# Attention followed by mixture of depths: own code for the last batch's MoE, and fewer, larger loads for the first two batches

## The chip, the cores and the metric

The kernel runs on one core of a Trainium2 chip. A core has TensorE (PE: matrix products and transposes into PSUM), VectorE (DVE), ScalarE (ACT), GpSimd (POOL, which here issues every DMA) and SyncE (SP, unused here). The engines run their own instruction queues in order and wait for each other by semaphores. The metric is the device time of one execution in microseconds (us); lower is better.

## The reference, cut to what matters

Eight batches, twelve heads, 448 tokens, 64 columns a head. The attention has no softmax: relu, then square. Its output, 768 wide, goes into a mixture-of-depths layer: the 128 tokens of each batch with the highest gate score get a two-layer network added, the others pass.

```python
scores = scale * np.matmul(q, k.transpose(0, 1, 3, 2))      # q, k, v: [8, 12, 448, 64]
attn = np.maximum(scores, 0.0) ** 2 / S
x = np.matmul(attn, v)                                       # then [8, 448, 768]
...
scores = np.einsum('bsd,d->bs', x, w_gate)
for b in range(B):
    top_idx = np.argpartition(-scores[b], capacity)[:capacity]      # capacity 128
    xe = x[b, top_idx]
    h = np.maximum(xe @ w1, 0.0)                                     # w1 [768, 1024]
    ye = h @ w2                                                      # w2 [1024, 768]
    g = 1.0 / (1.0 + np.exp(-scores[b, top_idx]))
    out[b, top_idx] = x[b, top_idx] + g[:, None] * ye
```

## The kernel before

**Attention.** The work goes by head pairs: 48 of them, t = 0 to 47, six to a batch (hp = 0 to 5). For a pair, `transposes(t)` turns q and k on TensorE into the PSUM tile `t_ps`, and VectorE copies them to `qkt`; `scores(t, c)` makes four chunks of scores in `s_ps`; `relu_square(t, c)` takes a chunk through ScalarE (`r_sb`) and VectorE (`a_sb`); `attend(t, c)` multiplies by v into `o_ps`, and ScalarE copies the result, transposed, into `xT_sb`. In the loop the transposes of the next pair and the attend of the last one stand between the scores of this one.

**Mixture of depths.** Batch b-1 is ranked during the six pairs of batch b, in twelve half steps placed by the table `RANK`, and batch b-2 goes through its network by the table `FFN`. The ranking: `gate` (scores of all tokens, in `sc_ps`, copied to `bc`), `columns` (the same as columns, and their split in three bf16 pieces in `tok`), four `x_chunk` (x transposed back into `x_sb`; after the last one a DMA writes the whole batch to `out`), four `rank_chunk` on VectorE, `one_hot` (`hot`), `select` (`sel_ps`, then `sel`, `idx` and `g` on VectorE) and two `gather` halves (`xe_ps`, copied by ScalarE to `xeT`). The network: `hidden` (`h_ps`, relu to `hT`) and `project` (`ye_ps`, scaled by the gate into `gye`); then a DMA on GpSimd adds the 128 rows of `gye` to `out` at the rows `idx`. After the last pair the same steps run for batches 6 and 7 with no attention beside them.

**PSUM.** Eight banks: `s_ps` has two tiles of two banks, `t_ps`, `o_ps`, `ma_ps` and `mb_ps` one bank each. All steps of the ranking use `ma_ps` one after the other (only the second gather half uses `mb_ps`), all of the network `mb_ps`.

**Order.** Within an engine the attention and the MoE steps stand in the order of the code (`manual_schedule`). The instructions ahead of the loop on VectorE that only prepare constants (`wg_rep`, the gate's weights spread out; `slot_row`; `tie`, the tie-breaker of the ranking; `tok`) are put into VectorE's queue by the framework, not by the code. GpSimd's queue holds every DMA in the order of the code; a DMA that it issues waits until the DMA eight places ahead of it has landed. `load(b + 2)` is issued at the first pair of batch b; the weights `w1_sb` and `w2_sb` are issued ahead of batch 2's loads.

**Loads.** q of some heads is one DMA; k and v are four DMAs each for any number of heads (even and odd heads, and the two halves of the tokens). The DMAs turn float32 into bf16.

Of the kernel before, what the change touches and what calls it, by code (L numbers as in the profile page):

```python
# [19 lines left out]
def kernel(  # L20
# [204 lines left out]
    def moe_rank(b):  # L225
        xTb = xT.pop(b)
# [80 lines left out]
    def moe_ffn(b, idx, g, xeT):  # L307
# [14 lines left out]
        def project(half, f0, f1):  # L322
            cols_d = slice(half * 384, half * 384 + 384)
            if f0 == 0:
                ps["y"] = mb_ps_pool.tile([CAP, 384], FP32, name="ye_ps", tag="m")
# [5 lines left out]
            if f1 == NF:  # L331
                nc.scalar.activation(out=gye[:, cols_d], in_=ps["y"], func=AF.Copy,  # L332
                                     scale=g[:, 0:1])
                if half == 1:
                    nc.gpsimd.indirect_dma_start(  # L335
                        out=out.rearrange("b s d -> (b s) d"),
                        out_offset=bass.IndirectOffsetOnAxis(ap=idx[:, :1], axis=0),
                        in_=gye, in_offset=None, element_offset=b * S * HD,
                        compute_op=ALU.add)

        return {"h": hidden, "y": project}


# [93 lines left out]
```

## Time and profile before

| | us |
|---|---|
| median of 3 runs (260.65 to 262.56) | 262.12 |
| the profiled execution's own time | 262.02 |
| its span, first to last instruction | 260.0 |
| so outside the span | 2.0 |
| TensorE busy, VectorE busy, ScalarE busy, GpSimd busy | 211.9, 180.8, 196.3, 93.4 |

The mean granted TensorE clock is 0.968 of full speed. Instants below are counted from the start of the span. Busy times overlap across engines, so they don't add up to the span; what a stage costs is read from what waits in it.

### The profile page before, as it was taken

The numbers are of one execution on the slowest core, as the hardware profiler recorded it, in microseconds if no ns is written. First come the engines' busy times: TensorE is split into PE (matmuls) and PEld (weight loads), VectorE is DVE, ScalarE is ACT, GpSimd is POOL, SyncE is SP. The second block draws the span as 40 slices with busy tenths as digits, with TensorE's granted clock in tenths as the row PEclk, the third lists the DMA queues.
The fourth block names the chain that finished last, engine by engine and source line by source line (L and its number), as shares of the span: only waits on it lengthen the run. The fifth ranks groups of instructions, "written<-read, shape, count | busy, mean of one in ns | idle before, by whom it ended". The sixth has DMA issues, their size and how long they took to land.

```text
span 260.0 us, 6204 instructions
## 1 busy us (share of the span) xinstructions
PE 211.9 (82%) x2496; PEld 128.0 (49%) x2496; DVE 180.8 (70%) x427; ACT 196.3 (76%) x306; POOL 93.4 (36%) x136
## 2 busy tenths in 40 slices
PE   1777795832989889998989898989899889988750
PEld 1343353411656445655565456546655556456630
DVE  4566879970478786889589958996798669847200
ACT  1667996950689989898989988898889889962320
POOL 8998998106473109200830074002000300020022
PEclk9988999995699999999999999999999999999997
DMA  3789999999999966995599549944102330153544
GB/s 41 90 84 110 160 159 149 211 204 193 196 227 279 191 222 80 189 117 212 70 185 128 210 62 173 151 159 87 32 3 115 105 58 0 63 159 55 212 61 61
DMA packets 41868, 34.20 MB, mean 132 GB/s; under 512 B 15089, under 2 KB 39153, under 8 KB 40945
## 3 DMA queue, kind: packets, MB, share of 16 engines
q0 software_dynamic: 41840, 33.83, 77.9%
q8 instruction: 19, 0.31, 0.5%
q14 instruction: 9, 0.07, 0.1%
HBM read 39.32 MB, written 14.16 MB: 206 GB/s over the span
## 4 chain that ended last, share of the span: by engine, by line
DVE 29%; PE 25%; DMA 14%; ACT 12%; POOL 12%; issue 5%; POOLq 1%; ACTq 0%
DVE a_sb L202 13%; ACT r_sb L201 11%; DMA k_sb<-in_k_dram 8%; DVE qkt L179 6%; PE xe_ps L297 5%; PE h_ps L316 4%; DMA q_sb<-in_q_dram 4%; DVE trash L273 4%; PE s_ps L189 4%; PE sc_ps L245 3%; DVE x_sb L268 3%; PE o_ps L213 3%; POOL k_sb L89 2%; DMA out_dram<-gye,idx 2%; POOL v_sb L92 2%
## 5 line engine op out<-in xcount | busy, mean ns | idle before, releaser
L201 ACT ACTIVATE r_sb<-s_ps 128x896 bf16<-128x896 f32 x192 | 147.5, 830 | 22.2 <-PE s_ps L193 13.7
L202 DVE TENSOR_TENSOR a_sb<-r_sb 128x896 bf16<-128x896 bf16 x192 | 104.3, 563 | 40.1 <-ACT r_sb L201 39.9
L189 PE MATMUL s_ps<-qkt 64*128 64x448 bf16 x288 | 47.0, 368 | 7.8 <-ACT r_sb L201 4.2
L213 PE MATMUL o_ps<-a_sb,v_sb 128*64 128x448 bf16 x384 | 49.8, 367 | 3.0 <-DVE a_sb L202 1.9
L179 DVE COPY qkt<-t_ps 128x960 bf16<-128x960 bf16 x48 | 31.3, 651 | 12.8 <-PE t_ps L174 12.6
L213 PEld LDWEIGHTS <-v_sb 128*64 128x64 bf16 x384 | 20.3, 110 | 29.9 <-issue 23.3
L270 POOL DMA_DIRECT2D out_dram<-x_sb x8 | 4.5, 561 | 78.9 <-DVE x_sb L268 78.4
L335 POOL DMA_INDIRECT out_dram<-gye,idx x8 | 13.4, 1674 | 43.5 <-ACT xeT L299 21.5
L219 ACT ACTIVATE xT_sb<-o_ps 128x448 bf16<-128x448 f32 x48 | 26.8, 559 | 2.3 <-PE o_ps L213 2.3
L316 PE MATMUL h_ps<-xeT,w_sb 128*128 128x128 bf16 x384 | 26.5, 219 | 1.3 <-ACT hT L320 0.7
L168 PE MATMUL t_ps<-ident,q_sb 112*64 112x112 bf16 x384 | 19.0, 221 | 10.2 <-DMA q_sb<-in_q_dram 10.2
L189 PEld LDWEIGHTS <-qkt 64*128 64x128 bf16 x288 | 11.4, 94 | 31.5 <-issue 18.0
L92 POOL DMA_DIRECT2D v_sb<-in_v_dram x24 | 18.5, 770 | 23.5 <-DMA q_sb<-in_q_dram 18.8
L168 PEld LDWEIGHTS <-q_sb 112*64 112x64 bf16 x384 | 16.9, 115 | 17.2 <-DMA q_sb<-in_q_dram 11.1
L329 PE MATMUL ye_ps<-w_sb,hT 128*128 128x384 bf16 x128 | 23.5, 327 | 2.1 <-ACT gye L332 1.1
L316 PEld LDWEIGHTS <-w_sb 128*128 128x128 bf16 x384 | 22.5, 98 | 5.1 <-issue 3.2
L174 PE MATMUL t_ps<-ident,k_sb 128*64 128x128 bf16 x384 | 21.4, 227 | 4.4 <-DMA k_sb<-in_k_dram 4.4
L89 POOL DMA_DIRECT2D v_sb<-in_v_dram x24 | 20.3, 845 | 12.6 <-issue 9.0
L273 DVE SCALAR_TENSOR_TENSOR trash<-bc,cols,tie 112x448 bf16<-112x448 f32 x32 | 21.7, 678 | 0.0
L265 PE MATMUL x_ps<-ident,xT_sb 128*112 128x128 bf16 x192 | 16.8, 224 | 5.6 <-DVE cols L256 5.5
L92 POOL DMA_DIRECT2D k_sb<-in_k_dram x24 | 20.0, 838 | 1.0 <-PE s_ps L193 0.6
L89 POOL DMA_DIRECT2D k_sb<-in_k_dram x24 | 20.1, 838 | 0.3 <-DMA v_sb<-in_v_dram 0.2
(54 smaller groups left out, 207.9 us busy)
## 6 DMA issues: line engine op xcount, KB each, us to landing
out_dram<-x_sb POOLq DMA_DIRECT2D x8, 1344.0 KB, 5.2
q_sb<-in_q_dram POOLq DMA_DIRECT2D x6, 672.0 KB, 9.5
w_sb<-in_moe_w_dram POOLq DMA_DIRECT2D x2, 1536.0 KB, 14.5
k_sb<-in_k_dram POOLq DMA_DIRECT2D x12, 192.0 KB, 10.5
v_sb<-in_v_dram POOLq DMA_DIRECT2D x12, 192.0 KB, 8.6
k_sb<-in_k_dram POOLq DMA_DIRECT2D x12, 144.0 KB, 10.3
v_sb<-in_v_dram POOLq DMA_DIRECT2D x12, 144.0 KB, 10.2
q_sb<-in_q_dram POOLq DMA_DIRECT2D x2, 336.0 KB, 4.9
```

Of the source, the lines that this page charges most:

```text
L89: nc.gpsimd.dma_start(out=t[0:64, hs, 0:lo, :], in_=src[b, hs, 0:64 * lo].rearrange("h (p c) d -> p h c d", c=lo))
L92: nc.gpsimd.dma_start(out=t[64:128, hs, 0:hi, :], in_=src[b, hs, 64 * lo:S].rearrange("h (p c) d -> p h c d", c=hi))
L168: nc.tensor.matmul(out=ps[64 * hh:64 * hh + 64, c * P:(c + 1) * P], lhsT=qs[:, h0 + hh, c, :], rhs=ident[:P, :P], is_transpose=True, start ...
L179: nc.vector.tensor_copy(out=sb, in_=ps)
L189: nc.tensor.matmul(out=ps[:, hh, :S], lhsT=sb[rows, S + c * 128:S + (c + 1) * 128], rhs=sb[rows, :S], start=True, stop=True)
L201: nc.scalar.activation(out=r[:, :n], in_=ps[:, :n, :S], func=AF.Relu)
L202: nc.vector.tensor_tensor(out=a[:, :n], in0=r[:, :n], in1=r[:, :n], op=ALU.mult)
L213: nc.tensor.matmul(out=o_ps[t][rows, :], lhsT=vs[:, 2 * hp + hh, c, :], rhs=a[:, hh if c < 3 else 0, :], start=(c == 0), stop=(c == 2), sk ...
L219: nc.scalar.activation(out=xT[b][:, hp, :], in_=o_ps.pop(t), func=AF.Copy, scale=o_scale)
L273: nc.vector.scalar_tensor_tensor(out=trash, in0=bc[:P, :], scalar=cols[:, c:c + 1], in1=tie[:, c, :], op0=ALU.subtract, op1=ALU.is_ge, acc ...
L316: nc.tensor.matmul(out=ps["h"][:, f % 4, :], lhsT=w1_sb[:, m, f * 128:(f + 1) * 128], rhs=xeT[:, m, :], start=(m == 0), stop=(m == NM - 1))
L329: nc.tensor.matmul(out=ps["y"], lhsT=hT[:, f, :], rhs=w2_sb[:, f, cols_d], start=(f == 0), stop=(f == NF - 1))
```

## The change

Three things. **The loads of the first two batches** are cut into fewer pieces: batch 0 in heads 0 to 1, 2 to 5 and 6 to 11 (before: 0 to 1, 2 to 3, 4 to 7, 8 to 11), batch 1 in one piece (before: two halves). **The last batch** leaves the tables: its gate, transposes, gather and network have functions of their own (`x_begin`, `x_end`, `gather_last`, `last`), which use the PSUM tiles that the attention has given up and mix batch 6's network with batch 7's ranking; the copies of x go to ScalarE as two of 1536 columns. **The gather halves** swap their banks for every batch: the first half now uses `mb_ps`, the second `ma_ps`, the bank that `select` has used just before. `pieces`, split off from `columns`, stands directly behind it in the loop.

```diff
-    load_q(0, 2, 4)
-    load_kv(k_sb, k, 0, 2, 4)
+    load_q(0, 2, 6)
+    load_kv(k_sb, k, 0, 2, 6)
     load_kv(v_sb, v, 0, 0, 2)
-    load_q(0, 4, 8)
-    load_kv(k_sb, k, 0, 4, 8)
-    load_kv(v_sb, v, 0, 2, 4)
-    load_kv(v_sb, v, 0, 4, 8)
-    load(0, 8, H)
+    load_kv(v_sb, v, 0, 2, 6)
+    load(0, 6, H)
     for i in range(1, NBUF):
         zero_halves(i)
-    load(1, 0, 6)
-
+    load(1, 0, H)
     wg_cols = const.tile([128, NM], BF16)
     nc.gpsimd.dma_start(out=wg_cols, in_=moe_w_gate.rearrange("(m p) -> p m", p=128))
-    load(1, 6, H)
...
         def gather(half):
-            xe = (ma_ps_pool, mb_ps_pool)[half].tile([128, 3, CAP], FP32, name="xe_ps", tag="m")
+            xe = (mb_ps_pool, ma_ps_pool)[half].tile([128, 3, CAP], FP32, name="xe_ps", tag="m")
...
+        def x_begin():
+            for i in range(2):
+                ps["x", i] = s_ps_pool.tile([P, 2, 1024], BF16, name="x_ps2", tag="s")
+                for u in range(2):
+                    for m in range(NM - 1):
+                        x_part(i, u, m)
+
+        def x_part(i, u, m):
+            c = 2 * i + u
+            nc.tensor.matmul(out=ps["x", i][:, u, m * 128:(m + 1) * 128],
+                             lhsT=xTb[:, m, c * P:(c + 1) * P], rhs=ident,
+                             is_transpose=True, start=(m == 0), stop=(m == NM - 1))
+
+        def x_end():
+            for i in range(2):
+                for u in range(2):
+                    x_part(i, u, NM - 1)
+                nc.scalar.copy(out=x_sb[:, 2 * i:2 * i + 2, :], in_=ps["x", i][:, :, :HD])
+            nc.gpsimd.dma_start(out=out[b].rearrange("(p c) d -> p c d", c=NC), in_=x_sb)
+
+        def gather_last():
+            for half, (pool, tag) in enumerate(((o_ps_pool, "o"), (t_ps_pool, "t"))):
...
+                (nc.scalar.copy if half == 0 else nc.vector.tensor_copy)(
+                    out=xeT[:, half * 3:half * 3 + 3, :], in_=xe)
...
+        def last():
+            nc.scalar.activation(out=g, in_=g, func=AF.Sigmoid)
+            for half in range(2):
+                h = s_ps_pool.tile([128, 4, CAP], FP32, name="h_ps2", tag="s")
+                for m0 in (0, 3):
+                    for ff in range(4):
+                        f = 4 * half + ff
+                        for m in range(m0, m0 + 3):
...
+                nc.scalar.activation(out=hT[:, f:f + 4, :], in_=h, func=AF.Relu)
+            y = [mb_ps_pool.tile([CAP, 384], FP32, name="y_ps2", tag="m"),
+                 t_ps_pool.tile([CAP, 384], FP32, name="y_ps3", tag="t")]
...
+            nc.scalar.activation(out=gye[:, :384], in_=y[0], func=AF.Copy, scale=g[:, 0:1])
+            nc.vector.tensor_scalar(out=gye[:, 384:], in0=y[1], scalar1=g[:, 0:1],
+                                    scalar2=None, op0=ALU.mult)
+            scatter()
...
+        last, prev = B - 1, B - 2
+        r, handed[last] = moe_rank(last)
+        f = moe_ffn(prev, *handed.pop(prev))
+        r["gate"](0, NM - 1)
+        r["x_begin"]()
         for c in (0, 1, 3, 2):
             attend(NT - 1, c)
-        for hs in range(12):
-            moe(B, hs)
-        ffn_steps[B - 1] = moe_ffn(B - 1, *handed.pop(B - 1))
-        for hs in range(12):
-            place(FFN, ffn_steps[B - 1], hs)
+        r["gate"](NM - 1, NM)
+        r["col"]()
+        for c in range(NC):
+            r["rank"](c)
+        r["hot"]()
+        r["x_end"]()
+        for i in range(8):
+            f["h"](i, *((mb_ps_pool, "m"), (t_ps_pool, "t"))[i // 4])
+        f["y"](0, 0, 8, mb_ps_pool)
+        r["pieces"]()
+        r["xe_last"]()
+        f["y"](1, 0, 8, ma_ps_pool)
+        r["sel"](o_ps_pool, "o")
+        moe_ffn(last, *handed.pop(last))["last"]()
```

GpSimd's queue at the second half of batch 1's loads, before (the sizes are partitions x heads x elements, `_97` to `_99` batch 1's tiles):

```order
L122 DMA wg_cols<-in_moe_w_gate_dram 128x6x1
L80 DMA q_sb_97<-in_q_dram 112x6x256
L89 DMA k_sb_98<-in_k_dram 64x3x256
L92 DMA k_sb_98<-in_k_dram 64x3x192
L89 DMA k_sb_98<-in_k_dram 64x3x192
L92 DMA k_sb_98<-in_k_dram 64x3x256
L89 DMA v_sb_99<-in_v_dram 64x3x256
L92 DMA v_sb_99<-in_v_dram 64x3x192
L89 DMA v_sb_99<-in_v_dram 64x3x192
L92 DMA v_sb_99<-in_v_dram 64x3x256
```

And the whole of batch 1's loads after:

```order
L80 DMA q_sb_97<-in_q_dram 112x12x256
L89 DMA k_sb_98<-in_k_dram 64x6x256
L92 DMA k_sb_98<-in_k_dram 64x6x192
L89 DMA k_sb_98<-in_k_dram 64x6x192
L92 DMA k_sb_98<-in_k_dram 64x6x256
L89 DMA v_sb_99<-in_v_dram 64x6x256
L92 DMA v_sb_99<-in_v_dram 64x6x192
L89 DMA v_sb_99<-in_v_dram 64x6x192
L92 DMA v_sb_99<-in_v_dram 64x6x256
L118 DMA wg_cols<-in_moe_w_gate_dram 128x6x1
```

The nine DMAs of a load now carry twelve heads, and `wg_cols` stands behind all of them, no longer between two halves. Ahead of `w1_sb` there are 37 DMAs in place of 55.

VectorE's queue around the first pair of batch 1, before (a line with x2 is two instructions; `qkt` marks a pair):

```order
L202 TENSOR_TENSOR a_sb<-r_sb 128x896 [waits Activation_49]
L128 COPY wg_rep<-wg_cols 128x768 [waits DMASW5_49]
L202 TENSOR_TENSOR a_sb<-r_sb 128x896 [waits Activation_49] x2
L179 COPY qkt<-t_ps 128x960 [waits PE_49]
L202 TENSOR_TENSOR a_sb<-r_sb 128x448 [waits Activation_49]
L202 TENSOR_TENSOR a_sb<-r_sb 128x896 [waits Activation_49] x2
L136 CAST slot_row<-slot_i 112x128 [waits Pool_49]
L202 TENSOR_TENSOR a_sb<-r_sb 128x896 [waits Activation_49]
L179 COPY qkt<-t_ps 128x960 [waits PE_49]
L256 COPY cols<-col_ps 112x4 [waits PE_49]
L142 TENSOR_SCALAR tie<-tie_i 112x1792 [waits Pool_49]
L152 CAST tok_193<-tok_i 112x4x2 [waits Pool_49]
```

And after, at the same pairs:

```order
L174 COPY qkt<-t_ps 128x960 [waits PE_49]
L197 TENSOR_TENSOR a_sb<-r_sb 128x448 [waits Activation_49]
L131 CAST slot_row<-slot_i 112x128 [waits Pool_49]
L197 TENSOR_TENSOR a_sb<-r_sb 128x896 [waits Activation_49]
L137 TENSOR_SCALAR tie<-tie_i 112x1792 [waits Pool_49]
L123 COPY wg_rep<-wg_cols 128x768 [waits DMASW4_49]
L147 CAST tok_175<-tok_i 112x4x2 [waits Pool_49]
L147 CAST tok_177<-tok_i 112x4x2
L197 TENSOR_TENSOR a_sb<-r_sb 128x896 [waits Activation_49] x2
L174 COPY qkt<-t_ps 128x960 [waits PE_49]
L251 COPY cols<-col_ps 112x4 [waits PE_49]
```

`wg_rep` and `tie` moved: `wg_rep` now comes one pair later, behind the last product of pair 6 and behind `tie`, which before stood two lines behind the copy of `qkt` of pair 8. The gate's first matmul, which on TensorE stands ahead of the scores of pair 7 in both kernels, reads `wg_rep`.

TensorE's queue at batch 6's gather, before (numbers tell the tiles apart):

```order
L189 MATMUL s_ps_4083<-qkt_4008 128x448 [waits Activation_49]
L189 LDWEIGHTS qkt_4008
L189 MATMUL s_ps_4083<-qkt_4008 128x448
L297 LDWEIGHTS x_sb_3686
L297 MATMUL xe_ps_4090<-hot_3692,x_sb_3686 128x128 [waits DVE_49]
```

And after, where the second gather half begins:

```order
L294 MATMUL xe_ps_4072<-hot_3674,x_sb_3668 128x128
L294 LDWEIGHTS x_sb_3668
L294 MATMUL xe_ps_4072<-hot_3674,x_sb_3668 128x128
L294 LDWEIGHTS x_sb_3668
L294 MATMUL xe_ps_4086<-hot_3674,x_sb_3668 128x128 [waits DVE_49]
```

The wait for VectorE's copy of `sel_ps` has moved from the first of the 24 gather matmuls to the thirteenth.

## Rows read from the trace of the kernel before

**Rows 1.** Windows view: busy time of each engine (xcount), clock, DMA share, GB/s.

```profile
3.00:18.00 15.00, 9.82 (x78) 4.45 (x80) 7.49 (x18) 7.51 (x11) 15.00 (x28) 1.00 0.79 87
18.00:39.00 21.00, 17.75 (x190) 8.98 (x187) 15.85 (x30) 19.22 (x30) 19.61 (x32) 0.92 1.20 137
...
42.00:49.00 7.00, 5.32 (x66) 2.94 (x65) 6.96 (x18) 4.57 (x8) 2.75 (x5) 1.00 1.12 209
...
59.00:64.40 5.40, 0.87 (x9) 0.50 (x9) 0.00 (x0) 0.00 (x0) 3.38 (x5) 0.50 1.50 193
```

**Rows 2.** Chain that ended last, 0 to 66 us: start, us, what.

```profile
7.48 0.52 POOL v_sb L89
...
38.29 0.80 POOL w_sb L155
...
42.12 0.66 POOL k_sb L92
...
43.38 20.93 DMA k_sb<-in_k_dram
```

**Rows 3.** Timeline at batch 2's first pair: start, us, engine, line, [idle before].

```profile
60.96 0.59 PE L168 MATMUL t_ps<-ident,q_sb 112*64 112x112 bf16 x8 [5.64 <-DMA q_sb<-in_q_dram]
...
65.09 0.66 DVE L179 COPY qkt<-t_ps 128x960 bf16<-128x960 bf16 x1 [8.54 <-PE t_ps L174]
...
68.74 0.71 PE L189 MATMUL s_ps<-qkt 64*128 64x448 bf16 x4
```

**Rows 4.** Waits view, 0 to 30 us: us in total, times, longest.

```profile
PE t_ps L168 <- DMA q_sb<-in_q_dram: 4.6, 1, 4.6
...
PE t_ps L174 <- DMA k_sb<-in_k_dram: 1.7, 4, 0.6
```

**Rows 5.** Timeline at batch 1's first gate.

```profile
33.20 0.61 DVE L128 COPY wg_rep<-wg_cols 128x768 bf16<-128x768 bf16 x1
...
34.87 1.31 PE L245 MATMUL sc_ps<-xT_sb,wg_rep 128*128 128x448 bf16 x6
...
36.06 0.63 DVE L202 TENSOR_TENSOR a_sb<-r_sb 128x896 bf16<-128x896 bf16 x1 [0.27 <-ACT r_sb L201]
...
39.58 1.32 DVE L142 TENSOR_SCALAR tie<-tie_i 112x1792 f32<-112x1792 int32 x1
```

**Rows 6.** Timeline at the boundary of batches 4 and 5.

```profile
148.08 0.65 DVE L179 COPY qkt<-t_ps 128x960 bf16<-128x960 bf16 x1
...
148.85 1.50 PE L297 MATMUL xe_ps<-hot,x_sb 112*128 112x128 bf16 x24 [0.81 <-DVE sel L287]
...
149.72 0.48 ACT L299 CAST xeT<-xe_ps 128x384 bf16<-128x384 f32 x1 [0.58 <-PE xe_ps L297]
...
150.28 0.55 PE L189 MATMUL s_ps<-qkt 64*128 64x448 bf16 x4
```

**Rows 7.** Timeline of the last 30 us.

```profile
229.95 0.95 PE L213 MATMUL o_ps<-a_sb,v_sb 128*64 128x448 bf16 x8
230.06 0.48 ACT L299 CAST xeT<-xe_ps 128x384 bf16<-128x384 f32 x1 [0.19 <-PE xe_ps L297]
...
231.17 1.30 PE L245 MATMUL sc_ps<-xT_sb,wg_rep 128*128 128x448 bf16 x6
...
233.72 0.49 PE L265 MATMUL x_ps<-ident,xT_sb 128*112 128x128 bf16 x6 [0.25 <-DVE cols L256]
...
240.45 0.57 POOL L270 DMA_DIRECT2D out_dram<-x_sb  x1 [7.37 <-DVE x_sb L268]
...
246.89 1.58 POOL L335 DMA_INDIRECT out_dram<-gye,idx  x1 [5.87 <-ACT hT L320]
...
253.33 1.56 POOL L335 DMA_INDIRECT out_dram<-gye,idx  x1 [4.86 <-ACT gye L332]
```

**Rows 8.** Groups by form on ScalarE: busy us, mean ns.

```profile
L201 ACT ACTIVATE r_sb<-s_ps 128x896 bf16<-128x896 f32 x144 | 126.5, 922 | 7.6 <-PE s_ps L189 7.0
L219 ACT ACTIVATE xT_sb<-o_ps 128x448 bf16<-128x448 f32 x48 | 26.8, 559 | 2.3 <-PE o_ps L213 2.3
```

More of the change, by code (lines that the diff above doesn't have):

```diff
@@ L225, in moe_rank @@
     def moe_rank(b):
[L226 removed]
+        xTb = xT[b]
         x_sb = x_pool.tile([P, NC, HD], BF16, name="x_sb")
@@ L256, in columns, with pieces @@
             nc.vector.tensor_copy(out=cols, in_=col_ps)
+        def pieces():
             nc.vector.tensor_copy(out=tk[:, :, 2], in_=cols)
@@ L299, in gather @@
             nc.scalar.copy(out=xeT[:, half * 3:half * 3 + 3, :], in_=xe)
+        def x_begin():
[17 more added lines that the diff above has]
+            for half, (pool, tag) in enumerate(((o_ps_pool, "o"), (t_ps_pool, "t"))):
+                xe = pool.tile([128, 3, CAP], FP32, name="xe_ps2", tag=tag)
+                for mm in range(3):
+                    m = half * 3 + mm
+                    for c in range(NC):
+                        nc.tensor.matmul(out=xe[:, mm, :], lhsT=x_sb[:, c, m * 128:(m + 1) * 128],
+                                         rhs=hot[:, c, :], start=(c == 0), stop=(c == NC - 1))
+                (nc.scalar.copy if half == 0 else nc.vector.tensor_copy)(
+                    out=xeT[:, half * 3:half * 3 + 3, :], in_=xe)
         steps = {
-            "gate": gate, "col": columns, "x": x_chunk, "rank": rank_chunk,
+            "x_begin": x_begin, "x_end": x_end, "xe_last": gather_last,
+            "gate": gate, "col": columns, "pieces": pieces, "x": x_chunk, "rank": rank_chunk,
             "hot": one_hot, "sel": select, "xe": gather,
@@ L334, in project @@
                 if half == 1:
[L335 to L341, printed above, removed]
+                    scatter()
[7 more added lines that the diff above has]
+                        for m in range(m0, m0 + 3):
+                            nc.tensor.matmul(out=h[:, ff, :],
+                                             lhsT=w1_sb[:, m, f * 128:(f + 1) * 128],
+                                             rhs=xeT[:, m, :], start=(m == 0 and ff == 0),
+                                             stop=(m == NM - 1), skip_group_check=True)
+                f = 4 * half
+                nc.scalar.activation(out=hT[:, f:f + 4, :], in_=h, func=AF.Relu)
+            y = [mb_ps_pool.tile([CAP, 384], FP32, name="y_ps2", tag="m"),
+                 t_ps_pool.tile([CAP, 384], FP32, name="y_ps3", tag="t")]
+            for f0 in (0, 4):
+                for half in range(2):
+                    for f in range(f0, f0 + 4):
+                        nc.tensor.matmul(out=y[half], lhsT=hT[:, f, :],
+                                         rhs=w2_sb[:, f, half * 384:half * 384 + 384],
+                                         start=(f == 0), stop=(f == NF - 1))
+            nc.scalar.activation(out=gye[:, :384], in_=y[0], func=AF.Copy, scale=g[:, 0:1])
+            nc.vector.tensor_scalar(out=gye[:, 384:], in0=y[1], scalar1=g[:, 0:1],
+                                    scalar2=None, op0=ALU.mult)
+            scatter()
@@ L347, with scatter @@
+        def scatter():
+            nc.gpsimd.indirect_dma_start(
+                out=out.rearrange("b s d -> (b s) d"),
+                out_offset=bass.IndirectOffsetOnAxis(ap=idx[:, :1], axis=0),
+                in_=gye, in_offset=None, element_offset=b * S * HD, compute_op=ALU.add)
+        return {"h": hidden, "y": project, "last": last}
     RANK = {
-        1: [("gate", 0, 6)], 2: [("col",)], 3: [("x", 0)], 4: [("x", 1), ("rank", 0)],
+        1: [("gate", 0, 6)], 2: [("col",), ("pieces",)], 3: [("x", 0)], 4: [("x", 1), ("rank", 0)],
@@ L394 @@
             moe(b, 2 * hp + 1)
+        last, prev = B - 1, B - 2
[3 more added lines that the diff above has]
+        r["x_begin"]()
         for c in (0, 1, 3, 2):
             attend(NT - 1, c)
-        for hs in range(12):
-            moe(B, hs)
-        ffn_steps[B - 1] = moe_ffn(B - 1, *handed.pop(B - 1))
-        for hs in range(12):
-            place(FFN, ffn_steps[B - 1], hs)
+        r["gate"](NM - 1, NM)
+        r["col"]()
+        for c in range(NC):
+            r["rank"](c)
[9 more added lines that the diff above has]
+        moe_ffn(last, *handed.pop(last))["last"]()
 _INS = ['q', 'k', 'v', 'moe_w_gate', 'moe_w1', 'moe_w2', 'moe_capacity']
```

18 lines of the change are left out of this document (9 added, 9 removed).

## The prediction

> **What bounds the kernel now.** I read the windows view first. From 3 to 18 us GpSimd is busy all of the time while the DMA engines move only 87 GB/s; from 18 to 39 us it is busy 19.6 of 21 us at 137 GB/s; from 42 us the rate is 193 to 209 GB/s and GpSimd is mostly idle [rows 1]. So the loads are limited by their issue until about 40 us, and by the transfers after that. The chain of waits says the same: GpSimd's issues one after the other, a one-head k or v piece 0.52 us, a six-head one 0.66 us, the first weights at 38.29, and then one DMA wait of 20.93 us for batch 2's k [rows 2]. That wait is where it hurts: TensorE starts batch 2's first transposes at 60.96 after 5.64 us of idleness, so it was free at 55.32, and VectorE, idle for 8.54 us, gets the pair's `qkt` at 65.09 [rows 3]. In 59 to 64.4 us the granted clock is 0.50, the lower level (1.2 GHz) [rows 1].
>
> From 70 to 230 us the batches repeat in about 26.75 us; there the chain runs through all three compute engines, and one of its steps is TensorE's 0.81 us wait ahead of the gather, for VectorE's copy of `sel` [rows 6]. That wait repeats at five batch ends (0.81 or 0.82 us each, gathers at 95.36 to 202.34).
>
> The last 20 us hang on three DMAs to `out` that wait for each other: x of batch 7 at 240.45, the scatter of batch 6 at 246.89, that of batch 7 at 253.33, 6.44 us apart both times, and the end 6.67 us later [rows 7]. Each waits until the one ahead has landed, and the row of three starts with the last copy into `x_sb`.
>
> **The loads, part by part.** 18 DMAs fewer stand ahead of the weights: 16 of k and v at 0.52 to 0.6 us, 2 of q that cost somewhat more, about 10.3 us together; the ones left grow by up to 0.14 us each, some 1.2 us. So the first weights are issued at 28 to 29 us in place of 38.29 [rows 2].
>
> Transfers: a batch of q, k and v is 2.06 MB in bf16. Up to 18 us issue still sets the pace, and I take 1.8 MB of batch 0 as moved by then (1.3 MB before, 15 us at 87 GB/s). The other 2.33 MB of the first two batches at 190 GB/s end at 30.3 us; for `wg_cols` with its many small elements, now behind batch 1, I allow 1.1 us. Before, the weights' first issue ended at 39.09, they began to move some 1.2 us later, and the last wait on k ended at 64.31 [rows 2], 24.0 us after that. So k of batch 2 is there at 31.4 + 24.0 = 55.4 us.
>
> Compute: TensorE was free at 55.32. Up to 30 us the transposes wait for q once, 4.6 us at the start, which stays, and for k 1.7 us in four waits [rows 4]. The larger first pieces land later than the small ones did, so I take half of these, 0.9 us, as gained (0 to 1.7). Against it stands VectorE's new order. `wg_rep` was ready at 33.81, and the gate at 34.87 did not wait. Now it stands behind the product that ends at 36.69 and behind `tie`: 36.69 + 1.32 + 0.61 = 38.62, so TensorE, with pair 7's scores queued behind the gate, waits 3.75 us longer [rows 5]. Of this 1.9 us come back (1.32 of `tie` and some 0.6 of the small casts no longer stand ahead of the products at 39.58). Net 1.85 us lost: TensorE free at 55.32 - 0.9 + 1.85 = 56.3, just behind the data, and `qkt` at about 57.0. **Gain 65.09 - 57.0 = 8.1 us.** Bounds: 10 us if the reordering hides in ScalarE's slack, 4 us if the loads come as late as 60 us.
>
> Clock: at 1.2 GHz it took 68.74 - 65.09 = 3.65 us from `qkt` to the next scores [rows 3], at full clock 150.28 - 148.08 = 2.20 [rows 6]. With no long stall the clock should not fall there: **1.45 us** (0 to 1.45).
>
> A rule speaks against this part. The trace shows a GpSimd that is busy 15.00 of 15 us with issues [rows 1]. The Trainium skill ("DMA: Bandwidth & Descriptors", section "Issuing engines are not separate DMA queues") says that the sequencer's time to initiate a DMA is usually small relative to the DMA itself; by that, fewer issues would give nothing, which is the second rival below. This trace disagrees with it for pieces of 24 to 64 KB.
>
> **The gather's banks.** The first half now goes to `mb_ps`, free since the network's last copy, and the wait for `sel` moves to the thirteenth matmul, 0.75 us later, when the copy is done. So the gather starts at the end of the scores, 0.81 us earlier. What could eat it is ScalarE, which copies the halves: it was idle 0.58 us ahead of the first and 0.19 ahead of the second [rows 6], 0.77 us in all. I take 0.7 us, at five batch ends and at batch 1's, which at full clock looks like them: **4.2 us** (0 if another engine takes over at once, 4.9 at most). `pieces` behind `columns` issues the same instructions in the loop: nothing.
>
> **The tail.** ScalarE's second gather copy can start some 0.2 us earlier and ends at 230.3 [rows 7]; the gate needs its bank. Then on TensorE: five gate matmuls of six, 1.08; 20 transposes at 0.49/6, 1.63; the last attend 0.9: 234.0. ScalarE's 0.56 copy [rows 8] and the sixth gate matmul: 234.9. From the gate's end to the transposes behind `columns` it took 233.72 - 232.47 = 1.25 us [rows 7], now about 1.0, as they don't wait for `cols`: 235.9, and 236.1 after two of four. Then two ScalarE copies of 1536 columns. No such copy is in the trace; 896 columns take 0.92 us [rows 8], so at most 1.58 by columns, and not under 1.2: x is complete at 238.6 to 239.3, its DMA at 238.9 to 239.6 in place of 240.45. **Gain 1.1 us** (0.8 to 1.5). The rest, ranking (hot at about 239.8), both networks and the gather, ends near 251 by the same durations, while the last scatter can't go before 253.33 - 1.1 = 252.2. So the separate banks of the network are worth nothing in time: the three DMAs cover them.
>
> **The sum.** 8.1 + 1.45 + 4.2 + 1.1 = 14.85 us off the span of 260.0: 245.15, and with the 2.0 us outside 247.2. The profiled execution's 262.02 is 0.1 below the median, so this stands for the median too.
>
> **The rivals.**
>
> *The first batches take more of it back.* TensorE's new pause at the gate is over 3 us long, and after the idle stretch of before the clock was at 0.50 [rows 1]; if it falls here too, a pair's steps cost 1.45 us more, as above. And pieces of four and six heads may reach pairs 1 and 3 late: the 0.9 us and as much again are lost. Together 8.1 becomes about 4.85: 250.5.
>
> *The loads are bound by the transfers.* The rule of the skill quoted above would have it so. Then batch 2's k lands when it did, and the loads' gain and the clock's are gone; the five gathers (3.5) and the tail (1.1) stay: 257.4. For it: in 59 to 64.4 us the engines were at their rate. Against it: 87 GB/s with the same elements from 3 to 18 us [rows 1].
>
> *The gather isn't on the path.* If ScalarE or VectorE sets the pace of a batch end after all, the banks give nothing: 247.2 + 4.2 = 251.4. Against it: the chain passes through the gather.
>
> *Slower: every large DMA leaves a gap.* At most eight DMAs are in flight, and from batch 1's q to batch 2's last k there are 17. If a DMA of twelve heads only starts once an older one has landed, each leaves a gap g, and k lands at 55.4 + 17 g. With the clock's 1.45 us lost as well, the whole change is gone from g = 0.85 us on; with 1.0 us k lands at 72.4, TensorE starts 16.1 us later than forecast, and the kernel takes 247.2 + 16.1 + 1.45 = 264.8. Against it: 206 to 209 GB/s from 42 to 59 us with DMAs of this size queued [rows 1].
>
> **How the numbers follow.** The forecast's case (245 to 249) has 0.6. Earlier loads or a cheaper reordering, 243 to 245: 0.08. The first rival 0.14, the third 0.08, the transfers' 0.06, the slower one 0.02, and 0.02 for something near no change. The range from 244.0 to 252.0 leaves out the transfers' case, the slower one and the far ends. About 1% is what a measurement of this kernel can tell from no change; all cases but the last two are faster by more: faster 0.95, same 0.02, slower 0.03.
>
> **What would show it.** The first weights issued near 28.5 us; DMA rates near 190 GB/s from about 18 us; batch 2's first `qkt` near 57, with no clock at 0.50 between 55 and 70; a pause of TensorE of over 3 us ahead of batch 1's gate; no wait ahead of the gathers and 26.0 to 26.1 us a batch; the last three DMAs still 6.4 us apart. I am wrong if k of batch 2 lands after 58, if the batch period stays at 26.75, or if the last scatter waits for its rows and not for the scatter ahead of it.

## The result, and the profile after

The changed kernel takes **249.69 us** (median of four runs, 249.47 to 251.06); the kernel before took 262.34 us beside it (four runs, 260.65 to 262.56). The ratio is 0.954, 95% interval 0.949 to 0.959: 12.65 us less. The forecast was 247.2 us, 2.5 us too fast. The span of the profiled execution went from 260.0 to 247.7 us, and this is where the two traces differ (the "second gate" is the gate of batch 1, which runs in the first pair of batch 2; instants are starts):

| from ... to | before | after | gain | forecast |
|---|---|---|---|---|
| start of the span to ScalarE's copy of the second gate | 72.95 | 64.22 | 8.73 | 10.25 |
| five batch periods from there | 134.88 | 131.50 | 3.38 | 3.5 |
| from there to the DMA of the last x | 32.62 | 30.79 | 1.83 | 1.1 |
| from there to the end | 19.55 | 21.19 | -1.64 | 0 |

ScalarE's copies that the first two lines count by, two of the kernel before and two of the changed one:

```profile
72.95 0.53 ACT L248 COPY bc<-sc_ps 128x448 f32<-128x448 f32 x1 [0.19 <-PE sc_ps L245]
207.83 0.53 ACT L248 COPY bc<-sc_ps 128x448 f32<-128x448 f32 x1 [0.16 <-PE sc_ps L245]
...
64.22 0.53 ACT L243 COPY bc<-sc_ps 128x448 f32<-128x448 f32 x1 [0.16 <-PE sc_ps L240]
195.72 0.53 ACT L243 COPY bc<-sc_ps 128x448 f32<-128x448 f32 x1 [0.16 <-PE sc_ps L240]
```

The windows view of the changed kernel (window, length, busy us of PE, PEld, DVE, ACT and POOL with their counts, PE clock, DMA share, GB/s):

```profile
3.00:18.00 15.00, 9.58 (x72) 4.32 (x73) 7.05 (x17) 6.65 (x10) 14.55 (x26) 1.00 0.97 109
18.00:30.00 12.00, 9.52 (x117) 4.92 (x118) 9.55 (x18) 11.96 (x19) 9.27 (x13) 1.00 1.37 173
...
39.00:42.00 3.00, 3.00 (x31) 1.19 (x29) 0.48 (x1) 1.93 (x3) 0.06 (x1) 0.74 1.13 209
...
59.00:64.40 5.40, 5.36 (x68) 3.33 (x65) 3.90 (x11) 5.03 (x9) 2.15 (x4) 1.00 1.49 199
```

GpSimd is still nearly full from 3 to 18 us (14.55 of 15), but the DMA engines move 109 instead of 87 GB/s [rows 1]. From 59 to 64.4 us, where TensorE was busy for 0.87 of 5.40 us at the lower clock (0.50), it now works almost all of the time (5.36 us) at full clock. In exchange the clock is at 0.74 from 39 to 42 us.

GpSimd's timeline (start, us, engine, line, operation, idle time before it and what ended it):

```profile
26.45 0.66 POOL L92 DMA_DIRECT2D v_sb<-in_v_dram  x1 [2.41 <-DMA q_sb<-in_q_dram]
...
30.21 0.84 POOL L150 DMA_DIRECT2D w_sb<-in_moe_w_dram  x1
...
41.95 0.66 POOL L92 DMA_DIRECT2D v_sb<-in_v_dram  x1 [5.77 <-DMA w_sb<-in_moe_w_dram]
49.44 0.66 POOL L89 DMA_DIRECT2D v_sb<-in_v_dram  x1 [6.84 <-DMA w_sb<-in_moe_w_dram]
```

The first weights are issued at 30.21 in place of 38.29 us [rows 2]. Behind them GpSimd waits 5.77 and 6.84 us for a landing: in the program each of its DMAs waits for the one eight places ahead, and the weights are 1.5 MB each.

The timeline at batch 0's gate, VectorE's constants and TensorE:

```profile
35.38 0.62 DVE L197 TENSOR_TENSOR a_sb<-r_sb 128x896 bf16<-128x896 bf16 x1 [0.15 <-ACT r_sb L196]
35.93 1.17 DVE L137 TENSOR_SCALAR tie<-tie_i 112x1792 f32<-112x1792 int32 x1
37.02 0.54 DVE L123 COPY wg_rep<-wg_cols 128x768 bf16<-128x768 bf16 x1
...
37.62 2.42 PE L240 MATMUL sc_ps<-xT_sb,wg_rep 128*128 128x448 bf16 x6 [3.36 <-DVE wg_rep L123]
```

The forecast pause is there, 3.36 us. What was not in the forecast's sum is the 2.42 us that the six gate matmuls take behind it; they took 1.31 before [rows 5].

Batch 2's first pair:

```profile
56.96 0.68 DVE L275 TENSOR_TENSOR hot<-slot_row,rank 112x512 bf16<-112x512 f32 x1
57.28 0.39 PE L163 MATMUL t_ps<-ident,q_sb 112*64 112x112 bf16 x8
...
57.56 1.15 DVE L197 TENSOR_TENSOR a_sb<-r_sb 128x896 bf16<-128x896 bf16 x2
...
58.63 0.65 DVE L174 COPY qkt<-t_ps 128x960 bf16<-128x960 bf16 x1
...
60.17 0.55 PE L184 MATMUL s_ps<-qkt 64*128 64x448 bf16 x4
```

There is no wait for q or k any more (5.64 us before [rows 3]): the data has landed when TensorE gets there at 57.28. From `qkt` to the next scores it takes 1.54 us in place of 3.65.

The boundary of two later batches:

```profile
137.88 1.71 PE L294 MATMUL xe_ps<-hot,x_sb 112*128 112x128 bf16 x24
137.99 0.65 DVE L174 COPY qkt<-t_ps 128x960 bf16<-128x960 bf16 x1
138.56 0.15 DVE L284 COPY sel<-sel_ps 128x5 f32<-128x5 f32 x1
...
139.52 0.55 PE L184 MATMUL s_ps<-qkt 64*128 64x448 bf16 x4
```

The gather starts without the 0.81 us of idleness [rows 6], and from `qkt` to the scores it is 1.53 us against 2.20. The gather itself takes 1.71 us in place of 1.50.

The end:

```profile
226.51 0.58 POOL L317 DMA_DIRECT2D out_dram<-x_sb  x1 [5.49 <-ACT x_sb L316]
...
232.57 1.58 POOL L396 DMA_INDIRECT out_dram<-gye,idx  x1 [5.48 <-ACT g L369]
...
236.38 0.62 DVE L391 TENSOR_SCALAR gye<-y_ps,g 128x384 f32<-128x384 f32 x1 [4.88 <-ACT gye L390]
...
239.58 1.56 POOL L396 DMA_INDIRECT out_dram<-gye,idx  x1 [5.43 <-issue]
```

The last rows are ready at 237.0, the last scatter goes at 239.58. So it does not wait for its rows but for the scatter ahead of it. But the steps from one DMA to the next are 6.06 and 7.01 us, and the end comes 8.1 us behind the last, where it was 6.44, 6.44 and 6.67 [rows 7].

### The profile page after: what moved, and what is told of

It reads as the page before. It is cut to its first block, busy times and chain, and to the rows that moved or that the text cites. A ratio compares the mean times of both kernels' runs of the same rounds, so it can differ in the third digit from the quotient of the medians.

```text
span 247.7 us, 6180 instructions
## 1 busy us (share of the span) xinstructions
PE 208.7 (84%) x2496; PEld 125.3 (51%) x2496; DVE 179.1 (72%) x425; ACT 196.8 (79%) x306; POOL 83.9 (34%) x118
## 4 chain that ended last, share of the span: by engine, by line
PE 34%; DVE 28%; ACT 19%; issue 7%; DMA 6%; POOL 2%; POOLq 1%; ACTq 0%
ACT r_sb L196 16%; DVE a_sb L197 14%; PE o_ps L208 6%; PE s_ps L184 6%; DVE qkt L174 5%; PE sc_ps L240 5%; PE xe_ps L294 4%; DVE trash L270 4%; PE h_ps L346 3%; DVE x_sb L265 3%; DMA out_dram<-gye,idx 2%; PE t_ps L169 2%; DMA out_dram<-x_sb 2%; PE s_ps L188 2%; PE x_ps L262 2%
## 5 line engine op out<-in xcount | busy, mean ns | idle before, releaser
L208 PE MATMUL o_ps<-a_sb,v_sb 128*64 128x448 bf16 x384 | 49.1, 364 | 1.4 <-DVE a_sb L197 0.3
L396 POOL DMA_INDIRECT out_dram<-gye,idx x8 | 14.2, 1781 | 43.3 <-ACT r_sb L196 27.0
L92 POOL DMA_DIRECT2D v_sb<-in_v_dram x20 | 15.6, 782 | 29.0 <-DMA q_sb<-in_q_dram 19.3
L346 PE MATMUL h_ps<-xeT,w_sb 128*128 128x128 bf16 x336 | 23.0, 219 | 0.0
L169 PE MATMUL t_ps<-ident,k_sb 128*64 128x128 bf16 x384 | 20.7, 224 | 2.1 <-DMA k_sb<-in_k_dram 2.1
L359 PE MATMUL ye_ps<-w_sb,hT 128*128 128x384 bf16 x112 | 20.6, 327 | 0.6 <-ACT hT L350 0.6
L346 PEld LDWEIGHTS <-w_sb 128*128 128x128 bf16 x336 | 19.6, 98 | 2.8 <-issue 1.2
L89 POOL DMA_DIRECT2D v_sb<-in_v_dram x20 | 17.1, 856 | 10.4 <-DMA w_sb<-in_moe_w_dram 6.8
L262 PE MATMUL x_ps<-ident,xT_sb 128*112 128x128 bf16 x168 | 14.8, 224 | 5.0 <-DVE cols L251 5.0
L188 PE MATMUL s_ps<-qkt 128*128 128x448 bf16 x48 | 17.4, 363 | 0.4 <-ACT r_sb L196 0.4
L92 POOL DMA_DIRECT2D k_sb<-in_k_dram x20 | 17.4, 874 | 0.6 <-PE h_ps L346 0.4
```

Source lines behind the costliest of these rows:

```text
L92: nc.gpsimd.dma_start(out=t[64:128, hs, 0:hi, :], in_=src[b, hs, 64 * lo:S].rearrange("h (p c) d -> p h c d", c=hi))
L188: nc.tensor.matmul(out=ps[:, 0, :S], lhsT=sb[:, S + 384:S + 512], rhs=sb[:, :S], start=True, stop=True)
L208: nc.tensor.matmul(out=o_ps[t][rows, :], lhsT=vs[:, 2 * hp + hh, c, :], rhs=a[:, hh if c < 3 else 0, :], start=(c == 0), stop=(c == 2), sk ...
L346: nc.tensor.matmul(out=ps["h"][:, f % 4, :], lhsT=w1_sb[:, m, f * 128:(f + 1) * 128], rhs=xeT[:, m, :], start=(m == 0), stop=(m == NM - 1))
```

## The experiments

Every kernel was timed in five rounds against the kernel before. Ratios are to that, with 95% intervals.

### The three parts, each alone

Each is the kernel before with one part of the change. `loads_only` has the new order of loads:

```diff
-    load_q(0, 2, 4)
...
+    load_q(0, 2, 6)
...
+    load(1, 0, H)
```

> The kernel before with the new loads alone. First theory (terms of the sum as the two traces now show them): TensorE's first qkt copy of batch 2 moves from 65.09 to about 58.6 us and the clock no longer falls there, 6.5 + 1.45 = 7.9 us, so 254.4 us. Rival, the loads only move the waiting to a later stage (the transfers would bound the first 60 us anyway): the gate of batch 2 comes where it came before and the time stays above 259 us. Second rival, nearly all of the gain is in the loads and the other two parts add nothing: 250 us.

Measured: 255.91 us against 261.98, ratio 0.977 (0.974 to 0.981), 6.1 us. The copy of the second gate comes at 65.74 us, 7.2 us earlier than before. Batch 2's first `qkt` and the scores behind it:

```profile
59.47 0.65 DVE L174 COPY qkt<-t_ps 128x960 bf16<-128x960 bf16 x1
...
61.68 0.55 PE L184 MATMUL s_ps<-qkt 64*128 64x448 bf16 x4
```

The scores come 2.21 us behind `qkt`. The periods stay at 26.75 us. So the loads are worth 5.6 us up to `qkt` (the expectation had 6.5) and 1.44 us of clock; no later stage takes it back, except the last three DMAs, which take 20.9 us from the first of them to the end in place of 19.55. The second rival falls too: the loads are about half of the gain.

`swap_only` has the gather's banks alone:

```diff
-            xe = (ma_ps_pool, mb_ps_pool)[half].tile([128, 3, CAP], FP32, name="xe_ps", tag="m")
+            xe = (mb_ps_pool, ma_ps_pool)[half].tile([128, 3, CAP], FP32, name="xe_ps", tag="m")
```

> The kernel before with the two PSUM banks of the gather exchanged and nothing else. First theory: each batch's wait of 0.81 us ahead of the gather goes, the period falls from 26.75 to 26.1 us, six times 0.65 is 3.9 us, so 258.4 us. Rival, the gather is not on the path while the loads are as before, or ScalarE takes the time back: 262.3 us, periods unchanged at 26.75 us.

Measured: 258.23 us, ratio 0.987 (0.983 to 0.991), 3.75 us. The second gate's copy is still at 73.0 us: at batch 1's end the gather runs at the lower clock, behind the wait for the loads, and there it did not wait for `sel` in the kernel before either (from `qkt` to the scores 3.66 us, before 3.65):

```profile
66.07 2.74 PE L297 MATMUL xe_ps<-hot,x_sb 112*128 112x128 bf16 x24
```

The five periods behind it take 131.55 us in place of 134.88. The gather is on the path.

`tail_only` has the last batch's code alone:

```diff
-        for hs in range(12):
-            moe(B, hs)
...
+        r["x_begin"]()
...
+        moe_ffn(last, *handed.pop(last))["last"]()
```

> The kernel before with the last batch's own code alone (loads and gather as before). First theory: the write of the last batch's x goes out 1.1 to 1.8 us earlier, and the three DMAs behind it stay serial (each waits for the one before to land), so the end moves by what the first of them moves, less what slower landings take back: 260.5 to 262.1 us. Rival, the separate banks shorten the path to the last scatter's rows and these decide the end: rows 2.6 us earlier, 259 us or less. Second rival, the DMAs of the new tail land later for a reason that lies in the new order: 262.3 us or more.

Measured: 260.57 us, ratio 0.994 (0.992 to 0.997), 1.4 us. GpSimd's timeline of this run:

```profile
238.59 0.58 POOL L322 DMA_DIRECT2D out_dram<-x_sb  x1 [5.28 <-ACT x_sb L321]
245.09 1.58 POOL L401 DMA_INDIRECT out_dram<-gye,idx  x1 [5.92 <-ACT hT L386]
251.40 1.56 POOL L401 DMA_INDIRECT out_dram<-gye,idx  x1 [4.74 <-DMA out_dram<-gye,idx]
```

The write of x is 1.86 us earlier than before, the scatters follow after 6.50 and 6.31 us, the end at 258.3 after 6.9: the end moves with the first of the three. The last rows are ready at 249.08 us, ahead of the last scatter, so they do not decide.

The three add up to 11.2 us; the whole change gave 12.65. The intervals are too wide to say that the rest is real. One piece of it can be seen, the 0.67 us at batch 1's end, which the new banks give only together with the new loads.

### Is GpSimd's time really the price? `pool_delay`

Five instructions that move no bytes (7.99 us together), on GpSimd ahead of batch 1's loads of the changed kernel:

```diff
+    for i in range(5):
+        d = const.tile([P, NC, S], INT32, name=f"delay{i}")
+        nc.gpsimd.iota(d, pattern=[[-P, NC], [1, S]], base=i, channel_multiplier=-1)
     load(1, 0, H)
```

> The changed kernel with five more iota instructions on GpSimd (1.65 us each, 8.25 us, no bytes moved) ahead of the loads of batch 1, about as much GpSimd time as the merged loads saved. First theory: the start is bound by GpSimd's issuing, so the first weights are issued near 38 us again and 5 to 7 us of the gain are lost: 254.5 to 257 us. Rival, the start is bound by the transfers and GpSimd has slack (it waited 2.86 us for landings ahead of the weights): the time grows by 1 us or less, 250.5 us.

Measured: 258.92 us, ratio 0.988 (0.985 to 0.992), 9.2 us slower than the changed kernel. Windows of this run:

```profile
18.00:30.00 12.00, 8.96 (x103) 4.29 (x101) 9.61 (x18) 11.99 (x18) 12.00 (x12) 1.00 0.47 56
30.00:39.00 9.00, 2.92 (x21) 1.30 (x22) 1.36 (x3) 1.15 (x3) 6.89 (x12) 0.56 1.50 193
```

The DMA engines run dry (56 GB/s) while GpSimd counts, TensorE waits for batch 1 (3.83 us for q and 2.80 for k), and its clock falls to half. The weights are issued at 37.19 us. It cost more than the first theory's 5 to 7 us; a clock that stayed down until past 49 us fits that, but no run separates it from the waits. By the Trainium skill ("DMA: Bandwidth & Descriptors", section "Issuing engines are not separate DMA queues") the sequencer's time to initiate a DMA is usually small relative to the DMA itself. This start is an exception: GpSimd's time is on the path, and 7.99 us of it without one byte cost 9.2 us.

### What holds batch 2's start? Two edits, alone and together

`consts_by_hand` takes VectorE's constants out of the scheduler's hands:

```diff
...
+            if t == 6:
+                wg_constant()
             scores(t, 2)
             relu_square(t, 2)
             moe(b, 2 * hp + 1)
+            if t == 6:
+                rank_constants()
```

> The changed kernel with VectorE's constants placed by hand: wg_rep ahead of the square of pair 6's third score tile, tie, slot_row and tok behind the gate. First theory: the gate of batch 0 can start at about 35.6 instead of 37.6 us, the clock falls less or not at all (gate 1.3 to 1.5 us instead of 2.42), and 2 to 3 us of it reach the end: 246.7 to 247.7 us. Rival, the pause was cover for transfers (batch 2's k lands at 53.9 us whatever the gate does) or later waits take it back: 249.7 us, within 0.7.

Measured: 249.92 us, ratio 0.954 (0.950 to 0.958): no gain. TensorE's timeline:

```profile
35.73 1.31 PE L234 MATMUL sc_ps<-xT_sb,wg_rep 128*128 128x448 bf16 x6 [1.36 <-DVE wg_rep L429]
...
56.54 0.38 PE L163 MATMUL t_ps<-ident,k_sb 128*64 128x128 bf16 x7 [1.58 <-DMA k_sb<-in_k_dram]
...
57.74 2.74 PE L288 MATMUL xe_ps<-hot,x_sb 112*128 112x128 bf16 x24
```

The pause shrinks, the gate runs at full clock, TensorE is at batch 2's first transposes by 54.23 us, and there it waits for k and pays with the clock (0.66 from 57 to 62 us; 2.74 us for the gather that takes 1.71). The rival holds: the pause was cover for the transfers. Only its 53.9 us was too early, as the last of k was there at 56.5.

`weights_later` loads q and k of batch 2 ahead of the weights and leaves VectorE as it was; `hand_and_later` does both:

```diff
-    nc.gpsimd.dma_start(out=w1_sb, in_=moe_w1.rearrange("(m p) f -> p m f", p=128))
-    nc.gpsimd.dma_start(out=w2_sb, in_=moe_w2.rearrange("(m p) f -> p m f", p=128))
...
-                load(b + 2, 0, H)
+                load_q(b + 2, 0, H)
+                load_kv(k_sb, k, b + 2, 0, H)
+                if t == 0:
+                    nc.gpsimd.dma_start(out=w1_sb, in_=moe_w1.rearrange("(m p) f -> p m f", p=128))
+                load_kv(v_sb, v, b + 2, 0, H)
+                if t == 0:
+                    nc.gpsimd.dma_start(out=w2_sb, in_=moe_w2.rearrange("(m p) f -> p m f", p=128))
```

> The changed kernel with q and k of batch 2 loaded ahead of the two weights (w1 behind k, w2 behind v), VectorE's constants as in the changed kernel. First theory: in the changed kernel the pause at batch 0's gate and the landing of batch 2's k end at about the same time, so taking the transfers out of the way alone gives nothing, since the pause still decides: 249.7 us within 0.7. Rival, the order of the transfers alone is what holds batch 2's start: 247.5 us or less. Second rival, the weights come too late for the feed-forward steps at about 62 us: 251 us or more.

> Both: VectorE's constants placed by hand (gate at 35.7 us, 1.31 us long, as in the run before this one) and q and k of batch 2 ahead of the weights. First theory: neither the pause nor the data holds batch 2's start, the wait of 1.58 us for k and the half clock behind it (2.74 us for 24 gather matmuls in place of 1.5) go, and about 3 us reach the end: 246.5 to 247.2 us. Rival, the weights land too late or the later batches' loads take it back: 249.7 us or more.

Measured: `weights_later` 250.37 us, ratio 0.955 (0.952 to 0.958), nothing gained (TensorE does not wait for k there, but the pause at the gate is still 3.29 us); `hand_and_later` **247.49 us**, ratio 0.944 (0.941 to 0.947), 2.2 us better than the changed kernel. TensorE in the latter:

```profile
37.34 1.31 PE L232 MATMUL sc_ps<-xT_sb,wg_rep 128*128 128x448 bf16 x6 [1.45 <-DVE wg_rep L427]
...
55.84 0.39 PE L155 MATMUL t_ps<-ident,q_sb 112*64 112x112 bf16 x8
56.04 0.42 PE L161 MATMUL t_ps<-ident,k_sb 128*64 128x128 bf16 x8
...
57.08 1.72 PE L286 MATMUL xe_ps<-hot,x_sb 112*128 112x128 bf16 x24
```

No wait for k, full clock. Two bounds lay on top of each other: the pause at the gate and the landing of batch 2's k. Either edit alone runs into the other.

`wg_ahead` adds to this the gate's weights ahead of batch 1's v:

```diff
-    load(1, 0, H)
+    load_q(1, 0, H)
+    load_kv(k_sb, k, 1, 0, H)
     wg_cols = const.tile([128, NM], BF16)
     nc.gpsimd.dma_start(out=wg_cols, in_=moe_w_gate.rearrange("(m p) -> p m", p=128))
+    load_kv(v_sb, v, 1, 0, H)
```

> The kernel with constants by hand and weights behind q and k of batch 2 (247.5 us), with the gate's weights loaded ahead of v of batch 1 in place of behind it. First theory: GpSimd then waits for a landing anyway (4.5 us), so the load costs nothing there, the gate's weights land before 34 us, the wait of 1.45 us ahead of batch 0's gate goes and the end comes 1.0 to 1.5 us earlier: 246.0 to 246.5 us. Rival, v of batch 1 is pushed back and the next pairs wait for it, or the wait shows up at the next landing: 247.5 us or more.

Measured: 247.45 us, ratio 0.944 (0.940 to 0.948), as without it. My theory was wrong about the place of the wait. VectorE and TensorE:

```profile
35.73 0.38 DVE L191 TENSOR_TENSOR a_sb<-r_sb 128x448 bf16<-128x448 bf16 x1
36.03 0.55 DVE L429 COPY wg_rep<-wg_cols 128x768 bf16<-128x768 bf16 x1
...
36.64 1.31 PE L234 MATMUL sc_ps<-xT_sb,wg_rep 128*128 128x448 bf16 x6 [1.36 <-DVE wg_rep L429]
```

The weights had landed at 31.5 us (9.9 us after their issue). `wg_rep` stood in VectorE's queue behind a square that ended at 36.1.

### The end of the run

`old_network` gives the last batch's network back its one bank:

```diff
-        moe_ffn(last, *handed.pop(last))["last"]()
+        n = moe_ffn(last, *handed.pop(last))
+        for hs in range(12):
+            place(FFN, n, hs)
```

> The changed kernel with the last batch's feed-forward network in the old form (one PSUM bank in turn for both halves of h and of y, both y copies on ScalarE); the rest of the own tail stays. First theory (the prediction's own step): the last scatter waits for the scatter before it, not for its rows, which are ready 2.6 us earlier, so the separate banks of the network are worth nothing as long as the old form costs less than that: 249.7 us within 0.7. Rival, the network is on the path to the end: the rows come 1.5 to 3 us later and so does the end, 251.2 to 252.7 us.

Measured: 251.08 us, ratio 0.957 (0.954 to 0.960), an interval that overlaps the changed kernel's. The traces separate better than the times, because the code up to the last gate is the same and yet that gate's copy is at 223.79 us here and at 222.18 there. From this copy to the end it takes 25.71 us with the old network and 25.52 with the new. The rows come 2.4 us later, and now just decide:

```profile
240.47 0.58 ACT L362 ACTIVATE gye<-ye_ps,g 128x384 f32<-128x384 f32 x1 [1.55 <-PE ye_ps L359]
241.52 1.56 POOL L396 DMA_INDIRECT out_dram<-gye,idx  x1 [5.84 <-ACT gye L362]
```

So the separate banks of the network make the rows 2.4 us earlier and the end 0.2 us.

`tail_split` puts the second of the two x copies on VectorE and moves both, with the transposes that they wait for, ahead of the ranks:

```diff
-                nc.scalar.copy(out=x_sb[:, 2 * i:2 * i + 2, :], in_=ps["x", i][:, :, :HD])
+                (nc.scalar.copy if i == 0 else nc.vector.tensor_copy)(
+                    out=x_sb[:, 2 * i:2 * i + 2, :], in_=ps["x", i][:, :, :HD])
...
         r["col"]()
+        r["x_end"]()
         for c in range(NC):
             r["rank"](c)
         r["hot"]()
-        r["x_end"]()
```

> The changed kernel with the second of the two copies of the last batch's x on VectorE, ahead of the ranks, in place of ScalarE. First theory: the three DMAs at the end are one chain, so what counts is when the first of them is issued; two copies of 1.39 us now run beside each other, it goes out about 1.4 us earlier (near 225.1 us) and the end with it: 248.3 us. The rows of the last scatter come about 1.4 us later (238.4 us), which is about when it can then go. Rival, the chain is not what ends the run, the ranks behind the copy push the rows back: 249.7 us or up to 251 us.

Measured: 249.20 us, ratio 0.950 (0.947 to 0.953); against the changed kernel that is not resolved. In the trace the DMA goes 3.54 us behind the copy of the last gate in place of 4.33, and the end 24.1 us behind it in place of 25.5; 0.8 us of that is the DMA, the rest are shorter steps behind it (6.05, 6.61 and 7.9 us), as unexplained as the longer ones. ScalarE's half of x, the later one, and the DMA:

```profile
224.17 1.44 ACT L316 COPY x_sb<-x_ps 112x1536 bf16<-112x1536 bf16 x1 [0.71 <-PE x_ps L308]
...
226.46 0.58 POOL L318 DMA_DIRECT2D out_dram<-x_sb  x1 [4.71 <-ACT hT L351]
```

The x was complete at 225.61 us, but the DMA went at 226.46; the trace names the `hT` relu behind the copy as its releaser. Why it waited for that is open.

`lane_shift` tries one explanation for the longer steps of the last three DMAs:

```diff
...
+            if t == 13:
+                for i in range(2):
+                    nc.gpsimd.dma_start(out=extra[i], in_=moe_w_gate[0:128].rearrange("(o d) -> o d", o=1))
```

> The changed kernel with two more DMAs of 256 bytes each in the middle of the run. In the kernels with the new loads the last three DMAs follow each other at 6.0, 6.8 to 7.0 and 7.9 to 8.1 us, in those with the old loads at 6.4, 6.4 and 6.7. Theory: it goes by the place in the rotation of the eight semaphores, which the smaller number of DMAs shifts by two; with two more the intervals are 6.4, 6.4 and 6.7 us again and the end comes about 1.4 us earlier, 248.3 us. Rival: it has another cause, the intervals stay: 249.7 us.

Measured: 250.67 us, ratio 0.958 (0.955 to 0.962); steps of 6.12, 7.04 and 7.9 us. The theory falls: the steps stay.

### The pieces together

`all_parts` is `wg_ahead` with `tail_split` and with `wg_rep` ahead of pair 6:

```diff
+            if t == 6:
+                wg_constant()
             scores(t, 0)
...
-            if t == 6:
-                wg_constant()
             scores(t, 2)
```

> Constants by hand, weights behind q and k of batch 2, the gate's weights ahead of v of batch 1, VectorE's wg_rep now ahead of the first square of pair 6 (in the run before, its weights had landed at 31.5 us while it stood behind a square that ended at 36.1 us, so the gate still waited 1.36 us for it), and the last x copies on two engines. First theory: the gate's wait was one of order on VectorE, not of landing, and goes now (1.4 us); the tail brings 0.5 to 1.4 us: 245.0 to 246.0 us. Rival, the squares behind wg_rep come later by its 0.55 us and pass the loss on, and nothing but the tail is left: 246.5 to 247.5 us.

Measured: **244.54 us** (244.23 to 247.54), ratio 0.931 (0.929 to 0.934): 18 us under the kernel before and 5 under the changed one. It is 2.9 us under `wg_ahead`, more than the first theory had; how that splits between the gate and the tail no run shows. The profiled execution is the longest of the six, 247.54 us: in it TensorE waited 1.50 us for batch 1's k at 31 us and ran at half clock behind that. Even so its gate starts straight behind the scores:

```profile
34.17 0.55 DVE L430 COPY wg_rep<-wg_cols 128x768 bf16<-128x768 bf16 x1
...
37.06 0.56 PE L178 MATMUL s_ps<-qkt 64*128 64x448 bf16 x2
37.55 1.54 PE L234 MATMUL sc_ps<-xT_sb,wg_rep 128*128 128x448 bf16 x6
```

`wg_rep` is ready at 34.72 us, and no wait for it is left: the gate's wait was one of order on VectorE.

## Why the prediction was right, and where it was off

**Loads.** The mechanism was right: issue bound the start, and the merged DMAs bought the time (`loads_only`, `pool_delay`). The size was off: 8.1 us forecast, 6.46 measured (65.09 to 58.63). The early waits gained 0.69 us by pair 7 (its `qkt` at 34.15 for 34.84) where 0.9 was forecast; pairs 1 and 2 did come 0.6 us late, much as a rival had it, but pair 4 was ahead again.

The step that failed is *"Of this 1.9 us come back ... Net 1.85 us lost: TensorE free at ... 56.3"*. TensorE was free at 57.28, so the reordering cost 1.96 + 0.69 = 2.65 us, 0.8 more. The 1.9 us did come back: at its end the gate was 3.86 us later than before (40.04 for 36.18), at 57.28 TensorE was 1.96 us later. What the sum lacked are the gate's own matmuls, which took 1.1 us longer than before: the clock fell behind the pause, as the first rival said. Another 0.65 us lie between the transposes and `qkt`: I took 0.7 us, it was 1.35, because VectorE, which idled there before, now had `hot` and two squares ahead of the copy.

The forecast of k's landing (55.4 us) was also 1.1 us too early: with the pause smaller, k came at 56.5 (`consts_by_hand`). Up to 18 us 1.64 MB had moved (15 us at 109 GB/s) and not the 1.8 that were taken, the next 12 us ran at 173 GB/s and not at 190, and the first weights went out at 30.21 us and not at 28 to 29: ahead of them GpSimd now waited 3.2 us for landings (2.41 of them ahead of the issue at 26.45), where it had waited 1.4. That the compute path ends *"just behind the data"* was right and is why neither repair alone gave anything.

These sizes come from one pair of traces. Kernels with the new loads and the same code up to there (`loads_only`, `tail_split`, `lane_shift`, `old_network`) have that `qkt` at 59.25 to 60.14 us, two with the old loads (`swap_only`, `tail_only`) at 64.28 and 64.68. By all of them the loads are worth 4.1 to 6.5 us up to there, so the term was too large by 1.6 us at the least.

**Clock.** 1.45 us forecast; `loads_only`, with the old banks, shows 2.21 us from `qkt` to the scores in place of 3.65, 1.44 us.

**Gather's banks.** 4.2 us forecast for six gathers. 3.38 in the five periods and 0.67 at batch 1's end (1.54 against 2.21 us) make 4.05; the rest is back by the second gate's copy. That 0.7 us a gather came out is in part luck. The forecast had the copy of `sel` done when the thirteenth matmul needs it, and booked a small loss on ScalarE. But twelve matmuls (0.75 us, half of a gather of 1.50) from 137.88 on would be done at 138.63, and the copy ends at 138.71, so the second half still waits for it: the gather starts 0.88 us earlier against `qkt` and takes 0.21 us longer, which leaves the 0.67. A seventh gather, in the last batch, waited for the same copy and was not in the sum:

```profile
228.52 1.50 PE L297 MATMUL xe_ps<-hot,x_sb 112*128 112x128 bf16 x24 [0.38 <-DVE sel L287]
```

**Tail.** 1.1 us forecast (0.8 to 1.5) and 1.83 measured up to the DMA of x. From the gather's start on it is 1.38 (240.45 - 228.52 = 11.93 us before, 226.51 - 215.96 = 10.55 after), inside the bounds; most of the rest is the seventh gather. That the separate banks of the network are worth nothing came out at 0.2 us.

**The three DMAs.** *"the last three DMAs still 6.4 us apart"* failed: 6.06 and 7.01 us, and 8.1 to the end; 1.64 us of the gain are given back. This was not in any term, and its cause stays open.

The misses add up: 1.64 (loads), less what the tail gained beyond its term, 0.73, plus 1.64 (DMAs) is 2.55, the 2.5 us between 247.2 and 249.69. That it closes so well is luck too, as the starts of kernels with the same code differ by up to 1.5 us.

**The rivals.** Bound by the transfers (257.4): no, by `loads_only` and `pool_delay`. The gather not on the path: no, by `swap_only`. A gap per large DMA: no, 173 to 209 GB/s from 18 us on. The first batches taking more back: half right: its clock fell, its late pairs were caught up.

## What to carry to other kernels

A start of many small loads on one queue is priced by the issuing engine's busy time; read it beside the DMA rate before merging, and look at what the saved time lets a scheduler move, here constants on VectorE in front of a gate. Where a repair gives nothing, ask which second bound lay under the first: the pause and the transfers had to be removed together for 2.2 us. Writes that wait for each other at the end make the first of them the one to hasten; what shortens the path to the last one's data counts only beyond the slack.
